# Pooled attention and a tanh-shrink layer on one core: group 2 as seven products, and another order of transfers in group 1

## The chip, the cores and the metric

The kernel runs on one core of a Trainium2 chip. The time is the device time of the program in microseconds (us). The engines are TensorE (PE, with its weight loads as PEld), VectorE (DVE), ScalarE (ACT), GpSimd (POOL) and SyncE (SP). SyncE only issues transfers here. Each engine works through its own instructions in order.

## The reference

```python
# q, k, v: (8, 8, 576, 64) float32;  w_in: (512, 2048);  w_out: (2048, 512)
k_p = k.reshape(B, H, 72, 8, D).mean(axis=3)
v_p = v.reshape(B, H, 72, 8, D).mean(axis=3)
scores = (1 / sqrt(D)) * q @ k_p.T                 # 576 x 72 for each head
attn = softmax(scores)
x = (attn @ v_p) -> rows of 8 heads x 64, (4608, 512)
h = x @ w_in
out = (h - tanh(h)) @ w_out                        # (4608, 512), float32
```

## The kernel before

The 4608 rows are worked in nine groups of 512. Groups 0 to 7 are the first 512 tokens of batches 0 to 7. The last 64 tokens of each batch (the tails, two batches to a block of 128) make up group 8. Group 0 has a part of its own, written out by hand; groups 1 to 8 are one loop over `g`.

In each turn of that loop, TensorE does the two large products of group `g`: 16 column blocks of `x @ w_in` (`h_mms`, L445, four matmuls of 128x512 to a block), and then the output product. Between these matmuls stand the small ones that make x of the next batch, `nb = g + 1`. A dictionary `plan` says after which unit of group `g` each piece stands: negative keys are the 16 column blocks, counted to the end, and keys from 0 are units of the output product. The pieces are

- "s": scores of a block of 128 tokens (`s_mms`, L311), row maximum and difference on VectorE (L323, L326),
- "e": the exponential on ScalarE (L362),
- "t": turning the weights by a DMA transpose, two blocks at a time (`e_turn_dma`, L371, tiles E and ET; El and ETl for a tail),
- "a": weights by values on TensorE (`av_mms`, L398), then the normalisation on VectorE (L419, L420),
- "x": turning x by a DMA transpose into `xT`, two blocks at a time (`x_turn_dma`, L428; `xTt` for a tail), which the first product of the next group reads.

The first product goes, two column blocks at a time, through ScalarE's tanh (L458) and a subtraction on VectorE (L459) into `gT`.

The output product has two forms. In the plain form it is 16 units of four matmuls of 128x512 (`o_mms`, L513): four row blocks, each copied out by ScalarE and stored (`o_store`, L535, L538). For the groups in `SEVEN` it is a Strassen-Winograd scheme of seven products in 14 units of eight matmuls of 128x256 (`product`, L591), with sums of `gT` (`g_sum`, L573) and of quarters of the weights. The sums of the weights are made once, by eight subtractions on VectorE (`w_sums`, L556), that the units of the plain groups pop off the list `w_ops`. A group in `SEVEN` has a plan of its own, `PLAN7`, in which the scores stand earlier and a tail's values (`tail_values`) go into the next group by way of `carry`.

Inputs for later batches come in by DMA on SyncE's queue, in the order in which the code issues them: keys, queries and values (`k_pieces`, `q_pieces`, `v_pieces`), and last tokens (`tail_pieces`). Keys are pooled on GpSimd (`pool_k`, L214 to L220), turned (`k_turn_dma`, L272, tile kT), and copied into the block layout `KB` (`k_place_kT`, L266). Queries are cast (`q_cast`, L280) and turned (`q_turn_dma`, L286, tile qT). Values are pooled into `VB` on GpSimd (`pool_v`, L229 to L256). Last tokens are cast by GpSimd (`tail_cast`, L184) and turned (`turn_tail`, L187). `stores` holds the output transfers until `run` issues them.

The PSUM banks are shared by hand: in a plain group the first product takes bank `i % 6`; in a group in `SEVEN` it takes the pairs (2, 3), (4, 5), (0, 1) in turn, while its scores stand in 6 and 7.

## Time and profile before

| | |
|---|---|
| median of 3 runs | 292.66 us (291.98 to 294.29) |
| profiled execution | 291.9 us, its span 290.2 us |
| TensorE busy | 279.5 us, 96% of the span |
| VectorE, ScalarE, GpSimd busy | 219.1, 150.5, 145.3 us |
| read from and written to HBM | 36.70 and 9.44 MB |

The profile shows one execution; its times count from the start of the span. A row of a timeline gives start, duration, engine, line and operation, and in brackets the idle time before it with what ended it. In the list of instruction groups the numbers behind the first bar are busy time in us and the mean of one in ns. A DMA row's first number is the time in which SyncE issues it; its landing is listed apart, as the time from issue to landing.

### The profile page before, as it was taken

The numbers are of one execution on the slowest core, as the hardware profiler recorded it, in microseconds if no ns is written. First come the engines' busy times: TensorE is split into PE (matmuls) and PEld (weight loads), VectorE is DVE, ScalarE is ACT, GpSimd is POOL, SyncE is SP. The second block draws the span as 40 slices with busy tenths as digits, with TensorE's granted clock in tenths as the row PEclk, the third lists the DMA queues.
The fourth block names the chain that finished last, engine by engine and source line by source line (L and its number), as shares of the span: only waits on it lengthen the run. The fifth ranks groups of instructions, "written<-read, shape, count | busy, mean of one in ns | idle before, by whom it ended". The sixth has DMA issues, their size and how long they took to land.

```text
span 290.2 us, 5474 instructions
## 1 busy us (share of the span) xinstructions
PE 279.5 (96%) x2154; PEld 179.4 (62%) x2163; DVE 219.1 (76%) x310; ACT 150.5 (52%) x226; POOL 145.3 (50%) x120
## 2 busy tenths in 40 slices
PE   6699999999999999999999999999999999999994
PEld 2489955444554455448944885488548854874583
DVE  6776876888857995599659975996599757935782
ACT  2686653366416841478366735783576336415630
POOL 7839873149411970882799279917930720010000
PEclk9999999999999999999999999999999999999999
DMA  7999999799989999888899788979622641011005
GB/s 224 231 282 273 206 263 249 149 339 270 219 224 252 328 245 175 291 228 203 166 246 292 205 173 228 304 221 165 201 48 44 95 167 21 1 75 73 0 2 145
DMA packets 84474, 54.56 MB, mean 188 GB/s; under 512 B 59904, under 2 KB 73344, under 8 KB 84448
## 3 DMA queue, kind: packets, MB, share of 16 engines
q1 hardware_dynamic: 77744, 45.17, 61.6%
q0 software_dynamic: 6320, 8.65, 14.2%
q10 hardware_dynamic: 384, 0.39, 0.5%
q8 instruction: 17, 0.28, 0.4%
q14 instruction: 9, 0.07, 0.1%
HBM read 36.70 MB, written 9.44 MB: 159 GB/s over the span
## 4 chain that ended last, share of the span: by engine, by line
PE 85%; DVE 6%; ACT 4%; DMA 2%; issue 1%; SPq 0%; ACTq 0%
PE PS L445 34%; PE PS L591 24%; PE PS L513 14%; PE PS L398 4%; PE PS L465 4%; PE PS L311 3%; DVE gT L459 3%; DMA q_raw<-in_q_dram 2%; PE PS L292 1%; DVE sh L326 1%; DVE mx L323 1%; ACT qT L701 1%; ACT t_sb L458 1%; ACT ET L381 1%; ACT E L362 1%
## 5 line engine op out<-in xcount | busy, mean ns | idle before, releaser
L445 PE MATMUL PS<-xT,w1b 128*128 128x512 bf16 x448 | 100.8, 379 | 0.0
L459 DVE TENSOR_TENSOR gT<-PS,t_sb 128x1024 bf16<-128x1024 f32 x64 | 76.8, 1219 | 28.8 <-ACT t_sb L458 28.8
L458 ACT ACTIVATE t_sb<-PS 128x1024 f32<-128x1024 f32 x64 | 65.6, 1025 | 45.6 <-PE PS L445 43.8
L445 PEld LDWEIGHTS <-w1b 128*128 128x128 bf16 x512 | 49.4, 98 | 55.2
L591 PEld LDWEIGHTS <-gT 128*128 128x128 bf16 x480 | 46.3, 98 | 5.9
L513 PE MATMUL PS<-w2b,gT 128*128 128x512 bf16 x183 | 44.7, 379 | 0.5
L591 PE MATMUL PS<-w2b,gT 128*128 128x256 bf16 x288 | 34.4, 272 | 0.0
L573 POOL TENSOR_TENSOR gT<-gT 128x1024 bf16<-128x1024 bf16 x8 | 16.8, 2120 | 29.1 <-DVE rden L419 29.1
L513 PEld LDWEIGHTS <-gT 128*128 128x128 bf16 x192 | 17.4, 98 | 17.4
L323 DVE TENSOR_REDUCE mx<-PS 128x8 f32<-128x576 f32 x35 | 26.2, 749 | 1.6 <-PE PS L311 1.6
L326 DVE TENSOR_TENSOR sh<-PS,mx 128x576 f32<-128x576 f32 x35 | 26.5, 757 | 1.2
L362 ACT ACTIVATE E<-sh 128x576 bf16<-128x576 f32 x31 | 21.2, 684 | 9.4 <-DVE sh L326 9.3
L420 DVE TENSOR_TENSOR x_sb<-PS,rden 128x512 bf16<-128x512 f32 x32 | 22.1, 692 | 1.1
L229 POOL TENSOR_TENSOR v_raw<-v_raw 128x1280 f32<-128x1280 f32 x6 | 17.4, 2900 | 7.9 <-DMA v_raw<-in_v_dram 7.8
L214 POOL TENSOR_TENSOR k_raw<-k_raw 128x1280 f32<-128x1280 f32 x6 | 17.4, 2903 | 4.0 <-DMA k_raw<-in_k_dram 4.0
L618 DVE TENSOR_TENSOR o_h<-PS,q_raw 128x256 f32<-128x256 f32 x20 | 8.5, 424 | 12.6 <-PE PS L591 11.1
L419 DVE RECIPROCAL rden<-PS 128x8 f32<-128x8 f32 x36 | 7.4, 204 | 14.0 <-PE PS L398 14.0
L625 POOL TENSOR_TENSOR o_h<-o_h,k_raw 128x512 f32<-128x512 f32 x5 | 6.4, 1271 | 21.3 <-DVE o_h L618 21.0
L535 ACT COPY o_h<-PS 128x512 f32<-128x512 f32 x10 | 5.8, 583 | 21.1 <-PE PS L513 21.1
L398 PE MATMUL PS<-VB,ET 128*128 128x130 bf16 (+2 forms) x192 | 16.3, 221 | 0.1
L465 PE MATMUL PS<-xT,w1b 128*128 128x128 bf16 x256 | 15.6, 219 | 0.3 <-ACT xT L437 0.3
L398 PEld LDWEIGHTS <-ET 128*128 128x128 bf16 x192 | 13.5, 98 | 2.9 <-ACT ET L381 0.3
(104 smaller groups left out, 364.0 us busy)
## 6 DMA issues: line engine op xcount, KB each, us to landing
k_raw<-in_k_dram SPq DMA_DIRECT2D x14, 512.0 KB, 6.0
q_raw<-in_q_dram SPq DMA_DIRECT2D x12, 512.0 KB, 6.9
v_raw<-in_v_dram SPq DMA_DIRECT2D x12, 512.0 KB, 4.8
out_dram<-o_h SPq DMA_DIRECT2D x10, 512.0 KB, 3.8
out_dram<-o_h SPq DMA_DIRECT2D x12, 256.0 KB, 3.1
w1b<-in_moe_w_in_dram POOLq DMA_DIRECT2D x4, 512.0 KB, 10.3
q_raw<-in_q_dram POOLq DMA_DIRECT2D x2, 1024.0 KB, 15.4
w2b<-in_moe_w_out_dram POOLq DMA_DIRECT2D x4, 512.0 KB, 11.2
```

The lines of the kernel that those rows point to most:

```text
L214: eng.tensor_tensor(out=r[:, :, 0:4, :], in0=r[:, :, 0:4, :], in1=r[:, :, 4:8, :], op=ALU.add)
L323: nc.vector.reduce_max(out=mx.rearrange("p k h o -> p k (h o)"), in_=sc, axis=AX.X)
L326: nc.vector.tensor_tensor(out=sh[:, :, :, :], in0=sc, in1=mx.to_broadcast([128, 2, 4, G]), op=ALU.subtract)
L362: nc.scalar.activation(out=E[:, e, :, :].rearrange("p t c -> p (t c)")[:, 0:NK], in_=sh.rearrange("p k h c -> p (k h c)"), func=ACT.Exp, s ...
L398: nc.tensor.matmul(PS[ps, banks[half], D1 * h : D1 * (h + s1 - s0)], lhsT=ET[:, t, c0 : c0 + (ps.stop - ps.start)], rhs=VB[kb][:, t, s0:s1 ...
L420: nc.vector.tensor_tensor(out=x_sb, in0=ps[:, :, :, 0:D], in1=rden.to_broadcast([128, 2, 4, D]), op=ALU.mult,)
L445: nc.tensor.matmul(PS[:, bank, :].rearrange("p (j c) -> p j c", j=R), lhsT=w1b[:, fb, i * 128 : (i + 1) * 128], rhs=xT_of(g)[:, :, fb, :], ...
L458: nc.scalar.activation(out=t_sb[:, :, :], in_=ps, func=ACT.Tanh)
L459: nc.vector.tensor_sub(out=gT[:, i : i + 2, :], in0=ps, in1=t_sb[:, :, :])
L465: mm = nc.tensor.matmul(PS[:, bank, 128 * n : 128 * n + 128], lhsT=w1b[:, fb, (4 * c + n) * 128 : (4 * c + n + 1) * 128], rhs=xT_of(0)[:, ...
L513: mm = nc.tensor.matmul(PS[:, bank, 0 : c1 - c0], lhsT=gT[:, i, tb * 128 : (tb + 1) * 128], rhs=w2b[:, i, c0:c1], start=(i == 0), stop=(i ...
L591: nc.tensor.matmul(ps, lhsT=A[:, i, 128 * b : 128 * b + 128], rhs=B_[:, i, :], start=(n in "24" and i == 0), stop=(i == NQ - 1), skip_grou ...
```

## The change

Group 2 joins the groups in `SEVEN`. With it, all eight sums of the weights are popped in group 1, at eight units in place of four, and batch 3's tail is cast at the start of group 2. That leaves group 1 as the only plain group in the loop, and what was a case for `g == 1` becomes the plan itself, with some pieces moved by a unit: blocks 2 and 3 of values from unit 10 to 9, the tail's values from 12 to 13. On SyncE's queue in group 1, values of batch 3 are issued at unit 3, before x's turns (they were issued at the end of the group); keys are turned at unit 9 (from 4) and queries at unit 10 (from 0), both behind x's turns; the last tokens are loaded behind keys and queries of batch 4. The turned keys are placed by ScalarE and not by GpSimd. Group 0 issues its four stores together; group 1 issues its first two with the third.

```diff
-SEVEN = (3, 4, 5, 6, 7, 8)
+SEVEN = (2, 3, 4, 5, 6, 7, 8)
...
             if g in SEVEN:
                 r += k_pieces(g + 2) + q_pieces(g + 2)
             else:
-                r += (v_pieces(g + 1) if g == 2 else []) + q_pieces(g + 2) + k_pieces(g + 2)
+                r += q_pieces(g + 2) + k_pieces(g + 2)
...
             o_store(0, u % 4, OB[u % 4], (se, ve)[u % 2])
-    run(stores, 2)
+    run(stores)
...
             plan = {
-                -12: [("s", 0)],
-                -9: [("e", 0)],
-                -8: [("s", 1)],
-                -5: [("e", 1), ("t", 0)],
-                -3: [("s", 2)],
+                -10: [("s", 0)],
+                -7: [("e", 0)],
+                -5: [("s", 1)],
+                -2: [("e", 1), ("t", 0)],
+                -1: [("s", 2)],
                 0: [("e", 2)],
                 1: [("s", 3)],
-                3: [("e", 3), ("t", 1)],
-                4: [("a", 0)],
-                5: [("a", 1), ("x", 0)],
+                3: [("e", 3), ("t", 1), ("s", 4)],
+                4: [("e", 4), ("t", 2)],
+                6: [("a", 0)],
+                7: [("a", 1), ("x", 0)],
                 9: [("a", 2), ("a", 3), ("x", 1)],
+                13: [("a", 4), ("x", 2)],
             }
-            if g == 1:
-                plan[-10], plan[-7], plan[-5] = plan.pop(-12), plan.pop(-9), plan.pop(-8)
-                plan[-2], plan[-1] = [("e", 1), ("t", 0)], plan.pop(-3)
             if tail is not None:
                 units.append((s_tail(tail), av_tail(tail), slot_tl))
-                plan[3].append(("s", 4))
-                plan[4] += [("e", 4), ("t", 2)]
-                if g == 1:
-                    plan[6], plan[7] = plan[4][:1], plan.pop(5)
-                    plan[4] = plan[4][1:]
-                    plan[10] = plan.pop(9)
-                plan[12] = [("a", 4), ("x", 2)]
...
-        if nb in (5, 7):
+        if nb in (3, 5, 7):
             tail_cast(tail)
...
-                if tail and n == (1 if g in SEVEN else 0):
+                if tail and n == 1:
                     turn_tail(tail)
...
             if qd == 3:
                 o_store(g, tb, 4 + tb % 2, se)
-                if g == 1 or tb > 1:
+                if tb > 1:
                     run(stores)
...
             if more:
-                if u == (0 if g == 1 else 3):
+                if u == 3:
+                    run(v_next)
+                if u == 10:
                     q_turn_dma(nb + 1)
-                if u == 0:
-                    run(stores)
-                if u == (4 if g == 1 else 9):
+                if u == 9:
                     k_turn_dma(nb + 1)
-                    k_place_kT(nb + 1, ge)
-                if u == 11 and nb % 2 == 0:
-                    run(tail_pieces(nb // 2))
-                    tail_cast(nb // 2)
+                    k_place_kT(nb + 1, se)
             if u == 13:
                 load_for(g + 1)
-            if u in (8, 9, 13, 14):
+                run(tail_pieces(nb // 2))
+            if u in (6, 7, 8, 9, 12, 13, 14, 15):
                 w_ops.pop(0)()
```

## The prediction

> **What bounds the kernel now.** I read the page first: the engines' busy time, the granted clock and the costliest group.
>
> ```profile
> span 290.2 us, 5474 instructions
> PE 279.5 (96%) x2154; PEld 179.4 (62%) x2163; DVE 219.1 (76%) x310; ACT 150.5 (52%) x226; POOL 145.3 (50%) x120
> PEclk9999999999999999999999999999999999999999
> L445 PE MATMUL PS<-xT,w1b 128*128 128x512 bf16 x448 | 100.8, 379 | 0.0
> PE 85%; DVE 6%; ACT 4%; DMA 2%; issue 1%; SPq 0%; ACTq 0%
> ```
>
> TensorE is busy for 96% of the span at the full clock, and 85% of the chain that ended last is its work. So time is won by taking matmuls out and lost wherever TensorE is made to wait. Next I cut the span at the first L445 matmul of each group (read off the chain in order of time) and asked for the busy time of each stretch. The columns are span, then PE, PEld, DVE, ACT and POOL.
>
> ```profile
> 53.97:85.60 31.63, 31.29 (x186) 15.62 (x188) 25.72 (x38) 14.81 (x18) 14.79 (x11) 1.00 0.96 252
> 85.60:116.90 31.30, 31.14 (x187) 15.61 (x188) 23.07 (x32) 15.35 (x19) 13.90 (x9) 1.00 1.00 244
> 116.90:145.36 28.46, 28.46 (x217) 19.65 (x216) 22.32 (x29) 16.92 (x26) 19.97 (x13) 1.00 0.89 221
> 145.36:174.83 29.47, 29.30 (x226) 19.74 (x224) 24.17 (x32) 18.03 (x28) 22.04 (x15) 1.00 0.89 229
> 174.83:204.04 29.21, 29.21 (x229) 20.11 (x228) 23.56 (x32) 17.43 (x28) 21.24 (x14) 1.00 0.91 226
> 204.04:233.00 28.96, 28.96 (x226) 19.82 (x224) 24.17 (x32) 16.32 (x26) 15.32 (x11) 1.00 0.44 95
> ```
>
> The rows are groups 1 to 6. Groups 1 and 2 run the plain output product; from 3 on it is the seven products. The last column but one is the DMA engines' share, and in groups 1 and 2 it is 0.96 and 1.00.
>
> **Part 1, group 2 in seven products.** The chain prices the two forms in the groups that do nothing beside them:
>
> ```profile
> 247.57 12.37 PE PS L591 x112
> 259.94 13.81 PE PS L445 x64
> ```
>
> The second row is 64 matmuls of 128x512 (the first product; the plain output product has as many of the same shape), the first is the 112 of 128x256 of the seven. The exchange gives 13.81 - 12.37 = 1.44 us. Whole groups say the same: group 6 is seven products with four blocks and a tail's scores, which group 2 becomes (28.96); group 5 carries a tail's values in, which group 3 becomes (29.21). Together 58.17, against 31.30 + 28.46 = 59.76 now. So -1.59 us, if both run as undisturbed as groups 5 and 6, whose PE is busy without a gap.
>
> The four weight sums that move from group 2 into group 1 are four more subtractions on VectorE. They are needed only by the first product of group 2, which is 14 us later. Their cover is VectorE's idle time, 31.63 - 25.72 = 5.91 us in group 1, for 4 x 0.69 = 2.8 us; without it, they would sit ahead of the normalisations, which part 2 follows.
>
> ```profile
> 76.29 0.69 DVE L420 TENSOR_TENSOR x_sb<-PS,rden 128x512 bf16<-128x512 f32 x1
> 78.83 0.69 DVE L556 TENSOR_TENSOR k_raw<-w2b,k_raw 128x1024 bf16<-128x1024 bf16 x1
> 80.21 0.21 DVE L419 RECIPROCAL rden<-PS 128x8 f32<-128x8 f32 x1 [0.69 <-PE PS L398]
> 81.30 0.69 DVE L420 TENSOR_TENSOR x_sb<-PS,rden 128x512 bf16<-128x512 f32 x1
> ```
>
> **Part 2, the end of group 1 on the DMA queue of SyncE.** This is where it is decided. SyncE issues in order, so I list what it does there now:
>
> ```profile
> 62.32 1.01 SPq L538 DMA_DIRECT2D out_dram<-o_h  x2
> 69.15 2.06 SPq L371 DMA_TRANSPOSE ET<-E  x1
> 71.31 1.94 SPq L286 DMA_TRANSPOSE qT<-q_bf  x1
> 74.96 1.34 SPq L371 DMA_TRANSPOSE ET<-E  x1
> 78.31 1.23 SPq L272 DMA_TRANSPOSE kT<-kd  x1
> 80.73 2.65 SPq L428 DMA_TRANSPOSE xT<-x_sb  x2
> 86.81 1.79 SPq L136 DMA_DIRECT2D v_raw<-in_v_dram  x2
> ```
>
> Queries and keys of batch 3 are turned at 71.31 and 78.31, both ahead of x. After the change the order is ET, values of batch 3 (three loads), the tail's ET, x, x, kT, qT, stores, the tail's x, keys and queries of batch 4, last tokens. The second turn of x is issued when VectorE has normalised the fourth block. TensorE reaches blocks three and four a unit earlier (0.86 us), but three weight sums (2.1 us) now stand ahead, where one or two fitted into gaps: starting each operation when the one before ends, from the first normalisation at 76.29, gives 81.6 to 82.0, the same place as now (81.30 + 0.69 = 81.99). Each turn keeps SyncE 1.2 us, qT 1.9 to 2.1, so kT is issued at about 83.1 and qT at about 84.4, which is 13 us later than now. Their landing times are:
>
> ```profile
> L286 SPq DMA_TRANSPOSE qT<-q_bf x5: 1907/2072/2469, 52.0 to 167.7; - x5
> DMA to landing us min/median/max: 4.3/4.4/5.5
> L272 SPq DMA_TRANSPOSE kT<-kd x5: 1201/1227/1267, 55.1 to 172.9; - x5
> DMA to landing us min/median/max: 2.6/2.6/3.5
> ```
>
> So kT lands at 85.7 to 86.6 and qT at 88.7 to 89.9. The values ahead of them can add to it. They go out from 76.3, when the ET of 74.96 is issued, the last of the three at about 77.5. Of the same three loads of batch 2 the last was issued at 57.45 and landed 4.7 us later, at 62.15, and the small turn behind them landed at 58.06 + 4.5 = 62.56:
>
> ```profile
> 57.45 0.51 SPq L142 DMA_DIRECT2D v_raw<-in_v_dram  x1
> v_raw<-in_v_dram SPq DMA_DIRECT2D x1, 128.0 KB, 4.7
> 58.06 1.22 SPq L187 DMA_TRANSPOSE tl_T<-tl_bf  x1
> tl_T<-tl_bf SPq DMA_TRANSPOSE x1, 4.5
> ```
>
> By this the values land at about 82.2 and the tail's ET at about 82.7, ahead of its use near 83.1. The queue goes on with x, x, kT and qT, 37 squares of 128x128. With 11 squares more, qT takes 1.8 us longer than kT, 0.16 us a square, so the 37 take 6 us and qT is there at 88.7 at the earliest by this count too. With the slowest kT and qT of the rows (0.9 and 1.1 us over their medians) it is 90.7. I take 89.6, near the middle, since both the queue and the slowest single turns speak for some delay.
>
> When does TensorE want qT? Group 2 begins at 85.60 if group 1 keeps its length, and as a group of seven it computes scores after three column blocks of its first product, where it now does after five:
>
> ```profile
> 85.60 4.32 PE PS L445 x20
> 146.86 0.89 ACT L266 COPY KB<-kT 64x288 bf16<-64x288 bf16 x2 [2.83 <-DMA kT<-kd]
> 148.88 1.23 DVE L459 TENSOR_TENSOR gT<-PS,t_sb 128x1024 bf16<-128x1024 f32 x1 [3.00 <-ACT t_sb L458]
> 165.24 1.05 PE L591 MATMUL PS<-v_raw,q_raw 128*128 128x256 bf16 x8 [0.17 <-DVE q_raw L573]
> 85.64 0.59 ACT L535 COPY o_h<-PS 128x512 f32<-128x512 f32 x1 [3.62 <-PE PS L513]
> 87.42 1.02 ACT L458 ACTIVATE t_sb<-PS 128x1024 f32<-128x1024 f32 x1 [1.19 <-PE PS L445]
> ```
>
> 12 of those matmuls take 2.59 us (4.32 x 12 / 20), so the scores are wanted at 88.19: with qT at 89.6, a stall of 1.4 us.
>
> The same stall is fed from the other side. ScalarE now places kT, in its own order: behind that wait stand two output copies (0.59 each) and the first tanh of group 2. With kT at 86.1: 0.89 + 1.18 + 1.02 us make the first subtraction on VectorE start at about 89.3, against 88.47 (87.42 + 1.02) now. Bank 4, which the third column block needs, is copied out by 87.6, wanted at 87.3. In group 4 the chain from the first subtraction (148.88) to the second half of product 7 (165.24) is VectorE's own work throughout, 16.36 us; 89.3 + 16.4 = 105.7, and TensorE would be there 19.9 us after the start less the 0.5 of group 4's loss, at 105.0. So 0.7 us from that side alone. The two overlap; the larger counts: +1.4, bounds 0.5 and 2.5. None is below nothing, since qT at its fastest is 88.7.
>
> **Part 3, the rest.** Four stores of group 0 go in one go instead of two and two: 0.5 MB more ahead of the ET of 69.15, which at group 1's 252 GB/s is 2.1 us of queue.
>
> ```profile
> ET<-E SPq DMA_TRANSPOSE x1, 4.0
> 75.65 0.36 PE PS L398 x6
> ```
>
> That ET landed 4.0 us after its issue, at 73.2, and its first reader is at 75.65. So the cover is 2.5 us, and I count nothing; without it, every microsecond of it is on the path. The values of batch 3 land 9 us sooner, but only GpSimd waits for them; no TensorE row does. Behind ScalarE's copies waits the store of the third block, and behind that store on SyncE stand the tail's x, keys, queries and last tokens of batch 4, from about 89 on. GpSimd's pooling of keys and ScalarE's query casts in group 2 wait for these, half a group later; I count nothing for it, and if that cover is gone the casts stand ahead of the last tanh. Group 3 now starts with kT placed by ScalarE, as group 4 does, which lost 29.47 - 28.96 = 0.5 us to it, group 5 nothing: +0.2, bounds 0 and 0.5.
>
> **Sum.** -1.59 + 1.4 + 0.2 = 0.0 (by the bounds -1.1 to +1.4) on the profiled execution of 291.9 us (span 290.2): about 291.9. The runs shown have a median of 292.66 and a lowest of 291.98, so the profiled one is at the fast end; I put the forecast at 292.3, between the two.
>
> [...]
>
> **Rivals.** (a) Forecast: a gain of 1.6 us is mostly paid back at the first scores of group 2: as median 291.5 to 293.1, chance 0.48.
>
> (b) The turns land in time. If qT lands by 88.2, as it would if squares overlap with their issue (kT lands 1.4 us after its issue ends), or 0.5 us later, at the fastest of its row, the sum is 291.9 - 1.59 = 290.3 to 290.8; as median 290.7 to 291.2. For it: SyncE's queue is otherwise empty then. Against: qT never took under 4.3. Chance 0.27. [...]
>
> (c) Slower: the values in front hold up the x turns. If the values and the tail's ET land 1 us later than I count, at 83.7, the second x (16 squares, 2.6 us) lands at 86.3, after the 85.60 at which the first product of group 2 wants it, kT at 87.1 and qT, 1.1 us slow as its slowest row, at 90.8: a stall of 2.6 us, and 0.5 in group 3, in sum +1.5: 293.4, as median 293.8. It decides for slower from a qT later than 89.6. For it: DMA share 0.96 and 1.00 here. Against: the loads that now stand there (batch 3's) have 10 us of slack behind them. Chance 0.20.
>
> (d) The change doesn't do what it says: VectorE sets the pace of group 2, so that it stays at 31.30 while group 3 gains the tail's values (29.21 - 28.46): +0.75, 292.7, as median 293.1. Against it: groups 3 to 6 do not show this. Chance 0.05.
>
> **How the numbers follow.** One per cent, 2.9 us, is about what a measurement of this kernel can tell from no change. No case gains that: even -1.59 with nothing lost is 0.5%, so faster 0.03. Slower by that needs a stall of over 4 us, or (c) with something more: 0.08. Within: 0.89. The range takes (b) and (c) in: 290.6 to 294.2.
>
> **What would show it.** Right: the first qT-fed score matmul of group 2 with an idle before it of about 1.4 us, released by the DMA of qT; ScalarE idle for kT at about 86; groups 2 and 3 together 59.8 us. Wrong: no idle there and the pair near 58.2 (b), or group 2's first product late (c). The forecast fails most simply if qT lands 1 us sooner or later than 89.6.

## The result, and the profile after

The changed kernel takes 295.23 us as median of ten runs (294.0 to 297.19), the kernel before 292.70 (291.93 to 294.29). The ratio is 1.0086, with an interval of [1.0058, 1.0114]: slower by 0.9%. The forecast of 292.3 was 2.9 us too low, and the upper end of its range, 294.2, was passed by 1.0 us.

The page of the kernel after, in three rows: span, engines, and the chain that ended last by engine.

```profile
span 293.5 us, 5595 instructions
PE 279.0 (95%) x2211; PEld 183.7 (63%) x2211; DVE 227.5 (78%) x316; ACT 154.0 (52%) x237; POOL 153.8 (52%) x121
PE 75%; DMA 10%; ACT 6%; DVE 4%; issue 2%; SPq 1%; ACTq 0%
```

TensorE is busy for 0.5 us less in a span that is 3.3 us longer, and the DMA's part of the chain has gone from 2% to 10%. The same cut by groups as before shows where (groups 1 to 4; columns as there, the last but one is the DMA share):

```profile
54.43:86.60 32.17, 31.67 (x189) 15.71 (x190) 28.12 (x41) 14.33 (x18) 17.48 (x12) 1.00 0.94 250
86.60:118.98 32.38, 29.31 (x226) 19.64 (x224) 27.52 (x34) 18.91 (x30) 18.82 (x12) 1.00 1.09 228
118.98:148.50 29.52, 29.40 (x230) 20.02 (x228) 23.55 (x32) 17.31 (x28) 21.25 (x14) 1.00 0.97 222
148.50:177.81 29.31, 28.95 (x224) 19.64 (x222) 24.41 (x33) 17.98 (x28) 21.69 (x14) 1.00 1.02 235
```

In group 2 TensorE works 29.31 us, 1.8 less than before, and still the group takes 32.38, 1.1 more than before. So 3.07 us of it are waits, where there were 0.16. The list of what TensorE waits for from 50 us on names them (total, times, longest, in us):

```profile
PE PS L311 <- DMA qT<-q_bf: 1.7, 1, 1.7
PE PS L398 <- DMA ET<-E: 1.4, 1, 1.4
PE PS L445 <- DMA xT<-x_sb: 0.7, 2, 0.4
PE PS L398 <- DMA ETl<-El: 0.3, 1, 0.3
PE PS L311 <- DVE sh L326: 0.2, 1, 0.2
```

And the timeline of TensorE has the three that fall into groups 1 and 2 (start, duration, in brackets the idle time before it):

```profile
84.06 0.72 PE L398 MATMUL PS<-VB,ETl 128*64 128x130 bf16 x12 [0.32 <-DMA ETl<-El]
...
90.87 0.42 PE L311 MATMUL PS<-KB,qT 128*128 128x144 bf16 x4 [1.67 <-DMA qT<-q_bf]
...
112.37 0.53 PE L398 MATMUL PS<-VB,ET 128*128 128x130 bf16 x6 [1.40 <-DMA ET<-E]
```

The first scores of group 2 wait 1.67 us for the queries' turn, as forecast. The 1.40 us at 112.37, where the third block of weights meets the values, stand in no step of the prediction. SyncE's rows show when both turns went out:

```profile
77.00 1.16 SPq L136 DMA_DIRECT2D v_raw<-in_v_dram  x2
78.21 0.48 SPq L142 DMA_DIRECT2D v_raw<-in_v_dram  x1
78.78 1.23 SPq L371 DMA_TRANSPOSE ETl<-El  x1
80.11 3.63 SPq L428 DMA_TRANSPOSE xT<-x_sb  x2
83.84 1.23 SPq L272 DMA_TRANSPOSE kT<-kd  x1
85.12 1.83 SPq L286 DMA_TRANSPOSE qT<-q_bf  x1
...
106.60 1.61 SPq L371 DMA_TRANSPOSE ET<-E  x1
```

The chain in order of time has both, with the time from issue to landing:

```profile
85.12 5.71 DMA qT<-q_bf
...
106.60 5.72 DMA ET<-E
```

The queries' turn is issued 0.7 us after the forecast time, but group 1 itself starts 0.6 us later in this trace (54.43 against 53.80), so by the group's own time it is late by 0.1. It needs 5.71 us, where the median before was 4.4. The turn of weights needs 5.72, where the turns at the same place in groups 3 to 6 of the kernel before landed after 3.4 to 3.8. Why these two turns are so late is the question that most of the experiments go after.

With a group's length taken as the time from its first L445 matmul to that of the next group, the loss from group 1 on is all in groups 1 to 3:

| group | 1 | 2 | 3 | 4 | 5 | 6 |
|---|---|---|---|---|---|---|
| before | 31.64 | 31.30 | 28.46 | 29.46 | 29.22 | 28.95 |
| after | 32.02 | 32.37 | 29.52 | 29.47 | 29.23 | 28.96 |
| the prediction's terms | 31.64 | 30.36 | 29.41 | as before | as before | as before |

Groups 1 to 3 take 93.91 us together, 2.51 more than before. Another 0.63 us of the 3.3 stand ahead of group 1; in a second trace of the kernel after, group 1 starts at 53.85, so that they aren't shown to be the change's. (The ends of the windows above were read off a few matmuls later, so that these lengths differ from theirs by up to 0.16 us.)

### The profile page after: what moved, and what is told of

Its sections match the earlier page's. It is cut to its first block, busy times and chain, and to the rows that moved or that the text cites. A ratio compares the mean times of both kernels' runs of the same rounds, so it can differ in the third digit from the quotient of the medians.

```text
span 293.5 us, 5595 instructions
## 1 busy us (share of the span) xinstructions
PE 279.0 (95%) x2211; PEld 183.7 (63%) x2211; DVE 227.5 (78%) x316; ACT 154.0 (52%) x237; POOL 153.8 (52%) x121
## 4 chain that ended last, share of the span: by engine, by line
PE 75%; DMA 10%; ACT 6%; DVE 4%; issue 2%; SPq 1%; ACTq 0%
PE PS L445 35%; PE PS L591 23%; PE PS L513 5%; PE PS L465 4%; PE PS L398 4%; DMA ET<-E 3%; PE PS L311 3%; DMA xT<-x_sb 2%; DMA q_raw<-in_q_dram 2%; DMA qT<-q_bf 2%; PE PS L292 1%; ACT q_bf L280 1%; DVE x_sb L420 1%; ACT E L362 1%; ACT t_sb L458 1%
## 5 line engine op out<-in xcount | busy, mean ns | idle before, releaser
L445 PE MATMUL PS<-xT,w1b 128*128 128x512 bf16 x448 | 100.8, 379 | 0.7 <-DMA xT<-x_sb 0.7
L445 PEld LDWEIGHTS <-w1b 128*128 128x128 bf16 x512 | 49.3, 98 | 56.2 <-issue 0.8
L591 PEld LDWEIGHTS <-gT 128*128 128x128 bf16 x560 | 53.9, 98 | 6.9
L591 PE MATMUL PS<-w2b,gT 128*128 128x256 bf16 x336 | 40.1, 273 | 0.0
L573 POOL TENSOR_TENSOR gT<-gT 128x1024 bf16<-128x1024 bf16 x10 | 21.0, 2121 | 32.8 <-DVE rden L419 32.8
L513 PE MATMUL PS<-w2b,gT 128*128 128x512 bf16 x128 | 30.6, 379 | 0.0
L618 DVE TENSOR_TENSOR o_h<-PS,q_raw 128x256 f32<-128x256 f32 x22 | 9.3, 423 | 13.5 <-PE PS L591 13.5
L625 POOL TENSOR_TENSOR o_h<-o_h,k_raw 128x512 f32<-128x512 f32 x6 | 7.6, 1274 | 21.4 <-DVE o_h L618 21.0
L513 PEld LDWEIGHTS <-gT 128*128 128x128 bf16 x128 | 11.5, 98 | 11.1
L311 PEld LDWEIGHTS <-qT 128*128 128x128 bf16 x128 | 10.0, 98 | 9.8 <-DMA qT<-q_bf 2.2
```

What stands on the lines that cost most here:

```text
L445: nc.tensor.matmul(PS[:, bank, :].rearrange("p (j c) -> p j c", j=R), lhsT=w1b[:, fb, i * 128 : (i + 1) * 128], rhs=xT_of(g)[:, :, fb, :], ...
L513: mm = nc.tensor.matmul(PS[:, bank, 0 : c1 - c0], lhsT=gT[:, i, tb * 128 : (tb + 1) * 128], rhs=w2b[:, i, c0:c1], start=(i == 0), stop=(i ...
L573: return eng.tensor_tensor(out=o, in0=x, in1=y, op=op)
L591: nc.tensor.matmul(ps, lhsT=A[:, i, 128 * b : 128 * b + 128], rhs=B_[:, i, :], start=(n in "24" and i == 0), stop=(i == NQ - 1), skip_grou ...
```

## The experiments

Some expectations name the theories by letters. A: the turns at the end of group 1 go out too late. B: batch 4's loads, now ahead of the turns of group 2, hold these up. C: the seven products are themselves the cost. D: the load on the DMA engines, stores above all, lengthens the turns. P: VectorE and GpSimd hinder each other. F: a packet of the queue that the profile calls instruction, taken for one that brings TensorE its instructions, lengthens the turn in flight. Q: it is only the order in SyncE's queue, and what each turn waits for there, that makes the turns late. The table gives the medians (before was 292.56 to 292.92 beside them), the ratios to the kernel before with their intervals, and the groups' lengths in the profiled execution.

| kernel | median us | ratio | groups 1, 2, 3, 4 |
|---|---|---|---|
| after | 295.23 | 1.0086 [1.0058, 1.0114] | 32.02, 32.37, 29.52, 29.47 |
| queries early | 293.89 | 1.0034 [1.0016, 1.0052] | 32.15, 31.23, 29.63, – |
| seven products alone | 294.31 | 1.0057 [1.0036, 1.0079] | 31.64, 32.42, 29.30, – |
| values of batch 4 behind | 296.67 | 1.0124 [1.0093, 1.0155] | 31.82, 33.00, 31.44, – |
| order alone | 294.95 | 1.0061 [1.0039, 1.0083] | 31.86, 32.59, 28.46, – |
| after, without stores | 294.06 | 1.0050 [1.0030, 1.0070] | 32.25, 31.58, 29.56, – |
| before, without stores | 292.72 | 0.9999 [0.9980, 1.0018] | 31.64, 31.29, 28.47, – |
| seven alone, without stores | 294.11 | 1.0055 [1.0034, 1.0077] | 31.63, 33.79, 29.22, – |
| keys and queries early | 294.80 | 1.0079 [1.0056, 1.0102] | 32.57, 31.73, 29.55, – |
| after, shifted by 64 | 294.79 | 1.0066 [1.0037, 1.0095] | 32.23, 29.93, 30.10, 29.83 |
| before, shifted by 64 | 293.93 | 1.0033 [1.0014, 1.0052] | 32.36, 31.29, 29.66, 29.37 |
| keys and queries early, shifted | 295.24 | 1.0080 [1.0051, 1.0108] | 32.96, 31.16, 29.68, 29.96 |
| after, shifted by 32 | 295.58 | 1.0094 [1.0068, 1.0120] | 35.75, 29.16, 30.28, – |
| after, shifted by 96 | 294.65 | 1.0066 [1.0042, 1.0089] | 32.02, 30.26, 29.56, 28.95 |
| values of batch 3 late | 296.98 | 1.0140 [1.0119, 1.0161] | 31.63, 35.48, 29.66, – |

### The parts of the change

**Queries turned early.** Only the queries' turn goes back to unit 0 of group 1.

```diff
+                if u == 0:
+                    q_turn_dma(nb + 1)
                 if u == 3:
                     run(v_next)
-                if u == 10:
-                    q_turn_dma(nb + 1)
```

> The changed kernel with one edit: queries of batch 3 are turned at unit 0 of group 1 (as before the change), not at unit 10 behind x's turns. Theory A (the queue of SyncE is late from the end of group 1 on, and the late turn of queries is the piece that makes it so): the 1.67 us idle before the first scores of group 2 goes, keys and queries of batch 4 are issued some 1.8 us sooner, and the 1.40 us idle before the third block of values in group 2 shrinks to under 0.5: about 292.5. Rival B (that second idle comes from the values of batch 4, which stand straight ahead of the second ET whatever came earlier): only the first idle goes, 293.5. Rival C (seven products in group 2 are themselves the cost): no change by more than 0.5 us, 295.

The wait for qT is gone and the median falls by 1.34 us, most of the 1.67, to near rival B's 293.5. So theory A holds for this one wait. The other stays, at the same place and with a turn issued at the same time (106.55):

```profile
111.85 0.53 PE L398 MATMUL PS<-VB,ET 128*128 128x130 bf16 x6 [0.99 <-DMA ET<-E]
```

It is therefore no consequence of the queries' stall.

**Seven products without the new order.** From the kernel before: group 2 in `SEVEN`, the eight weight sums in group 1, everything on SyncE as it was (batch 4's keys go ahead of its queries).

```diff
-SEVEN = (3, 4, 5, 6, 7, 8)
+SEVEN = (2, 3, 4, 5, 6, 7, 8)
...
-            if u in (8, 9, 13, 14):
+            if u in (6, 7, 8, 9, 12, 13, 14, 15):
```

> The kernel before with only group 2 put into the seven products and all weight sums made in group 1; the transfers in group 1 keep the order of before (queries turned at unit 0, keys at unit 4 and placed by GpSimd, values of batch 3 loaded at the end, stores in two and two). Theory A (the order is the cost, the products the gain): groups 2 and 3 together take 58.2 to 59 us, 1.0 to 1.6 less than before, no idle before the first scores: 291.2 to 291.8. Rival C (the products cost): groups 2 and 3 over 60 us, over 293.5. A third way: the values of batch 3 now come too late for a group of seven, GpSimd ends its pooling late, the tail's turn holds up SyncE, and there is an idle at the end of group 2: 292 to 293.

No stall of queries, and yet group 2 is not shorter: waits of 1.05 us for a turn of weights, 0.47 for a sum on GpSimd, 0.53 for x. With values of batch 3 loaded at the end of group 1, GpSimd pools them only from 94.69, and its keys then run beside VectorE's sums:

```profile
94.69 2.91 POOL L229 TENSOR_TENSOR v_raw<-v_raw 128x1280 f32<-128x1280 f32 x1 [12.32 <-DMA v_raw<-in_v_dram]
...
105.42 1.86 POOL L217 TENSOR_TENSOR k_raw<-k_raw 128x640 f32<-128x640 f32 x1
107.37 2.40 POOL L220 TENSOR_TENSOR kd<-k_raw 128x640 bf16<-128x640 f32 x1
```

The last two take 1.54 to 1.55 each in all groups of the kernel before. So the old order does not suit seven products either. The time is the one of rival C (over 293.5), but TensorE works 29.79 us in group 2, less than the 31.14 before; the rest are waits.

**The order without seven products.** From the kernel before: the transfers and the plan as in the kernel after, group 2 still plain.

```diff
-                if u == (0 if g == 1 else 3):
+                if u == 3 and g == 1:
+                    run(v_next)
+                if u == (10 if g == 1 else 3):
                     q_turn_dma(nb + 1)
...
-                if u == (4 if g == 1 else 9):
+                if u == 9:
                     k_turn_dma(nb + 1)
-                    k_place_kT(nb + 1, ge)
...
+                    k_place_kT(nb + 1, se if g == 1 else ge)
...
             if u == 13:
                 load_for(g + 1)
+                if g == 1:
+                    run(tail_pieces(nb // 2))
```

> The kernel before with only the new order of transfers in group 1 (values of batch 3 at unit 3, keys turned at unit 9 and placed by ScalarE, queries turned at unit 10, last tokens at the end, group 0's stores in one go); group 2 stays plain, with its scores after five column blocks. Theory A with the interplay (the order costs because a group of seven wants its scores 1.7 us sooner and its values 3 us sooner): 0 to +1 us against before, 292.7 to 293.7. If the order costs by itself whatever group 2 is: +2.5 us or more, 295. If nothing waits, 292.7.

A plain group 2 wants its first scores two column blocks later, and the wait for qT is gone. What comes in its place is a wait for the last tokens, which are now loaded behind everything else:

```profile
105.74 0.45 PE L311 MATMUL PS<-KB,tl_T 128*64 128x144 bf16 x8 [1.00 <-DMA tl_T<-tl_bf]
```

By the ratios the two parts cost 1.7 and 1.8 us by themselves and 2.5 together; neither is free.

**Values of batch 3 late, values of batch 4 behind.** Two kernels from the kernel after. In one, batch 3's values go out at the end of group 1 (unit 13), so that keys and queries have SyncE's queue for themselves. In the other, batch 4's values go out at unit 13 of group 2.

```diff
-                if u == 3:
-                    run(v_next)
...
             if u == 13:
+                run(v_next)
                 load_for(g + 1)
```

> The changed kernel with the values of batch 3 loaded at the end of group 1, ahead of keys and queries of batch 4 (as before the change), all else as changed. If the values ahead of x are what delays keys and queries: the turn of queries is issued at the same 85 us but lands under 4.6 us after it, the idle falls from 1.67 under 0.8. If not, it stays over 1.2. Either way the values come at 98 and later for a group that wants them pooled at 106, and GpSimd's pooling meets VectorE's sums in the products: group 2 stays over 32, 295 or more.

```diff
             if u == 13:
                 k_place_kT(nb + 1, se)
+                run(v_next)
                 load_for(g + 1)
...
-        if g > 1:
+        if g > 2:
             run(v_next)
```

> The changed kernel with one edit: in group 2 the values of batch 4 are loaded at unit 13, behind ET, x, keys, and not ahead of the second ET. Rival B (these 1.18 MB ahead of the second ET are the cause of its 5.7 us): that ET lands in under 4.5 us and the 1.40 us idle before the third block of values goes, the 1.67 us idle stays: about 293.9. Theory A (the queue is late from group 1 on): the idle shrinks only in part, 294.6. Loads that come this late may cost in group 3, which would show as an idle there.

Both are slower. Without the values in front the queries' turn is issued at 83.81, 1.3 us sooner, of which 0.75 is that group 1 starts sooner in this trace (53.68). It lands after 5.6 us, and the wait for it is still 1.38 us. So taking the values away doesn't take this wait away. By itself that doesn't clear them, since this turn too has an instruction packet beside it (at 85, in a table below). The list of waits shows what the late values cost instead, for values of batch 3:

```profile
PE PS L398 <- DMA ET<-E: 4.3, 3, 2.6
```

and for values of batch 4, where the turns of group 2 were to gain:

```profile
PE PS L398 <- DMA ET<-E: 2.3, 3, 1.2
```

Of these three, one is group 2's turn of the third block: it lands after 5.1 us and is waited for by 0.80 in place of 1.40. Theory B had it under 4.5 with no wait, so the values are at most a part of this cause. The other two are in group 3, where the values are now late.

**Keys and queries early.** The first of these experiments, and the keys turned at unit 4 and placed by GpSimd as before.

```diff
-                if u == 9:
+                if u == 4:
                     k_turn_dma(nb + 1)
-                    k_place_kT(nb + 1, se)
+                    k_place_kT(nb + 1, ge)
```

> The changed kernel with queries turned at unit 0 and keys at unit 4, placed by GpSimd, as before the change; values of batch 3 still ahead of x. Theory Q: with no turn behind x left but the tail's, all three idles at the start of group 2 go and the gain comes out, 291.5 to 292. Theory D: one idle is traded for another as in the run with queries early alone; groups 1 to 3 stay over 92.3 us, 293 to 294.

With no turn of batch 3's keys and queries left at the end of group 1 the wait for ET is still 0.93 us in group 2, and the tail's turn in group 1 is waited for longer (0.65). The median is 0.9 us worse than with the queries alone.

### Load on the DMA engines

Three kernels leave out the eight stores of groups 0 and 1: the kernel after, the kernel before as a control, and the seven products alone.

```diff
-        for r0, r1, dst in out_rows(g, tb):
+        for r0, r1, dst in out_rows(g, tb) if g > 1 else []:
```

> The changed kernel without the eight stores of groups 0 and 1 (2.1 MB; those rows of the output are not written), all else in place. Theory D (the 16 DMA engines are the bound from 54 to 118 us, where their share is 0.96 and 1.00 already before the change, so a group 2 that is 1.6 us shorter has nothing to run on): the load falls by some 7 us of their time, ET and the loads land sooner, the 1.40 us idle of group 2 goes and the idle for queries shrinks; groups 1 to 3 fall from 93.9 to under 92.3, 292.5 or less. Rival Q (a chain: VectorE's normalisation, then x, keys, queries in one queue): the queries are issued at 85 us as before whatever the engines carry, both idles stay within 0.5 us, 294.5 to 295.

> The control: the kernel before without the same eight stores (those rows are not written). TensorE waited for no DMA there, so both theories expect no change: groups 1 to 3 at 91.2 to 91.4 us, 292.2 to 292.8. If it gains over 1 us, leaving out stores does something else as well, and the run above has to be read against this one.

> Group 2 in seven products with the old order of transfers, without the same eight stores (those rows are not written). Theory D: with the DMA engines relieved the gain of the seven products comes out: groups 1 to 3 at 90.3 to 91, 291.2 to 291.8, against 93.36 with the stores. Rival P (the loss there comes from VectorE and GpSimd getting in each other's way in group 2, 1.22 us sums taking 2.4 us): it stays over 92.5, 293.5.

The control does not move (0.9999). The kernel after gains 1.2 us, but both waits stay: 1.43 us for qT and 0.86 for ET. They land after 5.5 and 5.2 us. So the stores take part, above all in the second wait, and are not the main cause: the 292.5 of theory D did not come. The seven products alone gain nothing measurable, and in their profile the largest wait is for GpSimd's sum, which had gone behind the late values and keys:

```profile
116.07 1.48 PE L591 MATMUL PS<-k_raw,gT 128*128 128x256 bf16 x12 [1.74 <-POOL gT L573]
```

That fits theory P, for the seven products in the old order only; how much of it is VectorE in GpSimd's way, and how much the late loads, is not shown. In the kernel after TensorE waits for no sum of GpSimd's.

### What lengthens the two turns

The queue "q8 instruction" has 17 packets of 16 KB (0.28 MB in all), in both kernels. The kernel after has 4422 TensorE instructions (2211 matmuls and as many weight loads), one packet for 260 of them if all are its own. In slices of 1 us, the traces show one packet in flight with each of the two long turns. Here are 85 to 91 us and 106 to 112.5 us of the kernel after (packets, MB, share; then transfer, count, us from issue to landing):

```profile
q8 instruction: 1, 0.02, 1.0%
...
qT<-q_bf SPq DMA_TRANSPOSE x1, 5.7
...
q8 instruction: 1, 0.02, 1.0%
...
ET<-E SPq DMA_TRANSPOSE x1, 5.7
```

The slices with a packet, in us of the span:

| kernel | packets at |
|---|---|
| before | 48 69 86 109 130 144 164 179 197 211 227 |
| after | 48 69 88 110 129 142 160 174 195 207 225 |
| after, shifted by 64 | 55 75 102 113 135 146 167 186 200 215 230 |
| before, shifted by 64 | 56 76 100 117 139 158 172 192 203 225 235 |
| after, shifted by 32 | 44 61 83 108 120 140 158 173 190 203 223 |
| after, shifted by 96 | 49 74 95 112 130 142 164 175 197 211 228 |
| values of batch 3 late | 48 69 85 111 130 144 163 175 197 209 228 |

The queries' turns, all of one size, can be set beside these times. In the kernel before they are issued at 51.99, 71.31, 106.77, 136.36, 167.70 and 194.37 us and land after 4.3, 4.4, 5.5, 4.7, 4.4 and 5.6 us. Packets fall into the third (109) and the sixth (197), and into no other. In the kernel after, the turn of 85.12 with the packet of 88 takes 5.7; four others take 4.3 to 4.8, one of them (138.52) with the packet of 142 in its last half microsecond. One is in between: the turn of 109.66 lands after 4.9, though the packet of 110 comes just behind its issue. That packet is also the one beside the late ET, which was issued 3 us earlier.

All twenty traces together say when a packet costs. Of their 120 turns of queries, 68 had no packet that began while they were in flight: they landed after 4.2 to 5.7 us, the median 4.4. In 22 a packet began 1.3 to 4.0 us after the issue: 4.6 to 6.7 us, the median 5.6, all but one over 5.2. In nine it began within the first 0.6 us, as with the turn of 109.66: 4.3 to 4.9, the median 4.4. (The other 21 had one later than 4.0 us, which a turn that lands early can't meet.) So a packet in the middle of the flight costs about 1.2 us, and one at its start next to nothing.

The busy share of the 16 DMA engines from 85 to 91 us, in 40 slices of 0.15 us, shows what happens. The first row is the kernel after; the second is the same kernel with its packets moved, as in the next experiment, out of this stretch (its third trace):

```profile
DMA  9999991006999999999999999900010001999999
DMA  9999991006999999999999999999999998999999
```

The rows are alike up to 88.9. Then the engines of the kernel after stand nearly idle for 1.2 us (88.9 to 90.1, at 0 to 34 GB/s where about 210 stood before), just behind the packet of 88, with the queries' turn still in flight. So the turn isn't slowed by a lack of engines; it is held. What holds it in the meantime, the profile doesn't show.

To move the packets and nothing else, 64 small matmuls were added to the ones that run at the start, while TensorE waits for its first data. With their weight loads that is 128 of the 260 instructions to a packet, about half its spacing.

```diff
-    fill(11, 7)
+    fill(3, 7)
+    for _ in range(72):
+        nc.tensor.matmul(
+            PS[0:64, 7, 0:64], lhsT=zeros[:, 0:64], rhs=zeros[:, 0:64], start=True, stop=True
+        )
```

> The changed kernel with 64 more small matmuls on zeros at the start (3 wide and 72 of 64 columns in place of 11 wide), while TensorE waits for the first loads. Nothing else changes, but every later 16 KB packet of the queue that the profile calls instruction comes 64 matmuls sooner. Theory F (such a packet, seen at 88 and 110 us, sits in the DMA engines while the queries' turn and the second ET are in flight and makes them land 1.2 to 1.5 us later): the packets come at about 74 and 103, the queries land 4.3 to 4.7 us after issue and the second ET in under 4.2, the idle of 1.67 falls under 0.7, that of 1.40 to 0 to 0.3, group 2 takes 30.7 or less instead of 32.4, and the time falls to 292.7 to 293.7. Rival Q (order of transfers alone): both idles stay within 0.4 us, 295.

> The kernel before with the same 64 small matmuls more at the start. Theory F: its packets, now at 109, 130, 144, 164 and 179, move to about 95, 116, 137, 157 and 169; the one at 137 meets group 3's second ET (wanted 0.5 us after it lands), the one at 169 the x turns of group 4: idles of 0.5 to 1.0 us appear in group 3 or at the start of group 5, and the time rises by 0.5 to 1.5 us, 293.2 to 294.2. Rival Q: no idle, 292.5 to 292.9.

With 64 matmuls of TensorE more ahead of them, the packets of 88 and 110 are now at 75 and 102, and that of 129 is at 113: 8 to 16 us sooner. qT, issued at 84.84, lands after 4.4 us, and its wait falls from 1.67 to 0.31. The ET of the third block lands after 4.6 and is not waited for at all:

```profile
86.18:116.11 29.93, 29.47 (x226) 19.52 (x224) 27.41 (x34) 19.00 (x30) 18.80 (x12) 1.00 1.05 242
116.11:146.21 30.10, 29.57 (x231) 19.94 (x230) 23.56 (x32) 17.33 (x27) 21.24 (x14) 1.00 0.84 222
```

Group 2 is 2.4 us shorter than in the kernel after, and TensorE's waits in it are down to 29.93 - 29.47 = 0.46 us. But groups 3 and 4 are 0.6 and 0.4 us longer, with new waits for ET (0.43 and 0.72). So the waits went as theory F had them, and the time did not: 294.79 is near rival Q's 295, and the intervals do not tell it from the kernel after.

In the kernel before it goes the other way. Its packets fell where turns had slack, and moved they do not: the ET of group 3 that meets the packet at 139 lands after 5.3 us where it took 3.7, and TensorE waits. From 135 to 142 us:

```profile
q8 instruction: 1, 0.02, 0.8%
...
ET<-E SPq DMA_TRANSPOSE x1, 5.3
```

```profile
141.30 0.53 PE L398 MATMUL PS<-VB,ET 128*128 128x130 bf16 x6 [1.02 <-DMA ET<-E]
```

The median of the kernel before rises by 1.0 us, as theory F had it, with nothing changed but 64 matmuls in an opening wait. Two more shifts of the kernel after, by 32 and by 96 matmuls, and the early turns shifted by 64:

> The changed kernel with 32 small matmuls more at the start. Theory F, from the places of the packets in the changed kernel (88, 110): they move to about 81 and 107. The one at 107 still meets the second ET of group 2 (issued 106.6), the one at 81 the tail's ET and x of group 1, the queries are clear: the idle for queries falls under 0.7, that for the second ET stays 0.7 or more, an idle of 0.6 or more stands before the tail's values or the start of group 2; group 2 takes 30.3 to 31.6. Rival (the shift by 64 helped for another reason, as a warmer or colder start): group 2 as with 64, 29.9.

> The changed kernel with 96 small matmuls more at the start. Theory F: the packets of 88 and 110 move to about 71 and 97, that of 129 to 114, where it meets the x turns of group 2. Both idles of group 2 go as with 64 (group 2 in 30.4 or less), and an idle of 0.4 to 1.0 stands at the start of group 3, for x. Rival: group 2 over 31.5.

> The version with queries turned at unit 0 and keys at unit 4, placed by GpSimd (294.8 as it was), with the same 64 small matmuls more at the start. Theory F: the second ET of group 2 no longer meets a packet at 109, its 0.93 us idle goes; the 0.95 us of waits on VectorE at 92 to 94 stay: groups 2 and 3 in 60.2 or less instead of 61.3, 293.2 to 294. Rival Q: no change, 294.8.

With either shift qT lands after 4.3 us and the ET of group 2's third block is not waited for; group 2 takes 29.16 and 30.26. With 32, the packet at 83 meets the tail's turn instead:

```profile
86.16 0.72 PE L398 MATMUL PS<-VB,ETl 128*64 128x130 bf16 x12 [2.04 <-DMA ETl<-El]
```

and group 1 takes 35.75. Part of that is not the wait itself: eight plain matmuls behind this wait took 3.42 us, where they take 1.89 elsewhere, with a granted clock of 0.85 between 80 and 90 us. Theory F had put a wait of 0.7 us or more before the third block here, and missed: the packet is at 108, 0.4 us behind the issue of that turn, which lands after 3.7 us all the same. That is the packet at the start of a flight, as above. With 96, a packet at 197 costs group 5 a wait of 1.04 us for an ET, beside 0.59 for a copy of keys, and the group takes 31.70 in place of 29.23; the wait for x that was expected at the start of group 3 did not come, since x, with the packet of 112 beside it, landed 0.1 us ahead of its use. With keys and queries early and the shift by 64, the wait for ET in group 2 is gone, and waits of up to 0.82 us for turns come up in other groups. Groups 2 and 3 take 60.84 us, where theory F had 60.2 or less, and the median is 295.24, where it had 293.2 to 294: no gain, as rival Q had it.

### Does a packet keep its place?

The profile of the shifted kernel after was the fastest of its twelve runs: 293.28 us, against a median of 294.79. So four more traces were taken, of the kernels as they are.

> The changed kernel once more, for a second trace. If the places of the instruction packets are fixed by the program (theory F in its strict form), the waits are those of the first trace: the queries' turn about 1.4 to 1.7 us before the first scores of group 2, a turn of weights about 1.4 us at the third block of values, span 293 to 294. If they drift by a few microseconds from execution to execution, one of the two waits is under 0.5 us and another turn is waited for.

> The changed kernel with the 64 extra matmuls at the start once more. Its first trace had 291.6 us of span, while the median of its executions is 1.5 us higher. Strict F: again 291.6, group 2 at 29.9, groups 3 and 4 at 30.1 and 29.8. Drifting packets: a span of about 293, with other turns waited for in groups 1 to 5, 1 to 2 us more in sum.

> The same kernel a third time, to tell a drift from a single odd trace: strict F gives the same waits in all three, drift gives three different sets with spans between 291.6 and 295.

> The kernel before once more. Strict F: no wait of TensorE for a turn over 0.3 us, groups 1 to 3 at 91.4 us in sum, span 290 to 291. Drift: a wait of up to 1 us appears in one of the groups 3 to 8, while groups 1 and 2 stay, since their turns are issued long before they are wanted.

The packets keep their places within about 1 us (87 and 110 in the kernel after; 102 and 114, then 103 and 113 shifted); in the kernel before they differ by up to 2.3. In the kernel after both waits come again, behind landings of 5.5 and 5.7 us:

```profile
90.59 0.42 PE L311 MATMUL PS<-KB,qT 128*128 128x144 bf16 x4 [1.61 <-DMA qT<-q_bf]
...
112.29 0.53 PE L398 MATMUL PS<-VB,ET 128*128 128x130 bf16 x6 [1.56 <-DMA ET<-E]
```

In the shifted kernel qT lands after 4.4 us in all three traces, and its wait is 0.31, 0.38 and 0.35. Group 2 is not the same each time. Its rows in the second and the third trace:

```profile
86.31:117.69 31.38, 29.72 (x226) 19.51 (x224) 29.09 (x35) 19.00 (x30) 19.47 (x13) 1.00 1.02 236
```

```profile
86.45:116.74 30.29, 29.30 (x226) 19.59 (x225) 27.74 (x34) 19.07 (x30) 18.76 (x12) 1.00 1.07 241
```

The packet at 102 to 103 now meets the turn of the first two blocks, issued at 97.62 to 97.93. It lands after 7.3 to 8.1 us, where it took 6.2 in the kernel after, and is waited for by 0.64 us in the third trace. In the second trace TensorE waits for VectorE there (0.60 and 0.29 us). So strict F is right for the kernel after, and for the shifted one only in the place of its packets. Group 2 takes 30.53 us as mean of three, 1.9 less than the 32.45 of the kernel after's two traces; groups 3 and 4 take 60.0 against 59.0. Over groups 1 to 4 the net is 0.8 us; it agrees in sign with the medians, which differ by 0.44.

Before, traced again, had one wait of 0.52 us for an ET in group 2, where neither reading expected any. The packets account for it as theory F would: in the first trace that ET landed at 108.91, just ahead of the packet of 109.1; in the second, issued 0.3 us later, it met the packet at 108.8 and landed after 5.36 us in place of 3.55.

## Why the prediction was wrong

**The time, step by step.** Its terms give 91.41 us for groups 1 to 3; measured were 93.91. Of the missing 2.50, group 2 has 2.01, group 1 0.38, group 3 0.11. The 2.01 are 1.40 for the turn of weights, 0.27 more for the queries, and 0.34 by which TensorE's own work in group 2 (29.30) is longer than group 6's (28.96).

**Part 1, right in the exchange of products.** TensorE's busy time in group 2 falls by 1.8 us, where 2.2 would reach group 6's 28.96. Where the shifts take the two long waits away the group is at 29.2 to 31.4 us. The gain is there and is paid away.

**Part 2, right in place, short by 0.3, and near in part by luck.** The wait at the first qT-fed scores was put at 1.4 us and is 1.67 and 1.61 in two traces. kT was put at 86.1, and ScalarE's copy of it starts at 86.49. Counted from the start of group 1, qT was issued 0.1 us later than forecast and took 0.5 longer than the 5.2 us from 84.4 to 89.6; but group 2, which wants it, also began 0.4 later, and the two errors nearly cancel. The landing time was taken from its row of 4.3, 4.4 and 5.5 us as a scatter, to be met by a value in the middle. By the packets' times it isn't scatter: the 5.5 is the turn of 106.77, with the packet of 109 beside it. Read that way, the row had two prices, and the question was where the next packet falls. In the shifted kernel, at the lower price, the wait is 0.3 to 0.4 us.

**The step that failed: the turns of weights in group 2, counted at nothing.** Part 1 took the gain "if both run as undisturbed as groups 5 and 6", whose PE is "busy without a gap". Part 3 ("half a group later; I count nothing for it") looked at GpSimd and ScalarE as those that wait in group 2, and never at the turns of weights there. Group 2's ET of the third block is issued at 106.60, wanted at 110.97 and lands at 112.32. It had 4.37 us. The 3.4 to 4.6 us of the shifted traces would have cost 0.2 at most; 5.72 costs 1.40. No row was quoted for the cover of this turn, and there was next to none. The kernel before shows it: in its groups 3 to 6, all in seven products, the turn at this place was wanted 4.2 us after its issue and landed after 3.4 to 3.8. That is 0.4 to 0.8 us of cover, in group 3 by these rows (issue, landing, first reader):

```profile
135.05 1.27 SPq L371 DMA_TRANSPOSE ET<-E  x1
ET<-E SPq DMA_TRANSPOSE x1, 3.7
139.25 0.52 PE L398 MATMUL PS<-VB,ET 128*128 128x130 bf16 x6
```

None of these four turns met a packet in the middle of its flight. Another turn of weights in group 3 did (issued at 127.69, the packet of 130), and landed after 5.0 us; it had 7.35 us, so that nothing waited.

**Group 1, taken as unchanged.** The tail's turn is issued at 78.78, behind three loads of values, and is waited for by 0.32 us in both traces of the kernel after. The sum of "about 82.7, ahead of its use near 83.1" left 0.4 us of cover. The turn took 5.2 us, 0.7 more than the 4.5 that was counted.

**The side chain of VectorE, right in time for another reason.** The first subtraction of group 2 was put 3.7 us after the group's start (89.3 against 85.60; the terms given add up to 89.2), behind ScalarE's copy of kT. It starts at 90.16, 3.7 us after 86.45. But ScalarE's tanh had ended at 89.44. What stands ahead of the subtraction on VectorE is three weight sums, which are in no term of this chain. They run beside GpSimd's pooling of values:

```profile
85.67 1.35 DVE L556 TENSOR_TENSOR k_raw<-w2b,k_raw 128x1024 bf16<-128x1024 bf16 x1
86.94 2.03 DVE L556 TENSOR_TENSOR v_raw<-w2b 128x1024 bf16<-128x1024 bf16 x1
88.89 1.34 DVE L556 TENSOR_TENSOR v_raw<-w2b,k_raw 128x1024 bf16<-128x1024 bf16 x1
90.16 1.21 DVE L459 TENSOR_TENSOR gT<-PS,t_sb 128x1024 bf16<-128x1024 f32 x1
```

```profile
86.55 1.88 POOL L232 TENSOR_TENSOR v_raw<-v_raw 128x640 f32<-128x640 f32 x1
88.50 1.19 POOL L235 TENSOR_TENSOR v_raw<-v_raw 128x320 f32<-128x320 f32 x1
```

They take 4.72 us; three at the 0.68 to 0.69 us that each takes in the kernel before would take 2.0 to 2.1. No wait of TensorE in group 2 is put down to VectorE in the kernel after. Where qT is in time, there are such waits near 106 us: 0.28 and 0.28 with the queries early, 0.60 and 0.29 in one trace of the shifted kernel. Whether they come from these sums isn't shown.

**The rivals.** (b), turns in time, is what the shifts come near to in group 2. (c) came nearest in its time, with 293.8, but not by its cause: x landed at 85.80, ahead of the 86.45 at which it was wanted, and in the shifted kernel, with the values where they are, qT lands after 4.4 us. (d) did not happen. The chance of 0.89 for a change within 1% came true, at its edge, but not by the small terms that it stood on; and the measurement tells 0.9% from no change, where the prediction thought one per cent was the least.

**What stays open.** The shifts move waits as the packets would have it, in both kernels and both directions, and that a packet can lengthen the turn in flight by 1.1 to 1.6 us is shown by that. Why the engines then stand idle is open. And the medians follow the packets' places only in part: no shift of the kernel after comes within 1.5 us of the kernel before. The groups of seven products have little slack around their turns wherever a packet falls, and whether some place of the packets would leave all of them free was not found. Nor is it known how much of the 1.2 us without stores is queueing and how much the turns' own rate. A kernel with fewer TensorE instructions in groups 1 and 2, hence, at one for about 260, fewer packets, wasn't tried. No version beat the kernel before.

## What to carry to other kernels

A DMA turn that is issued 4.1 us ahead of its reader, with a landing time of 4.4 us, isn't hidden (the queries' turn of the shifted kernel after, waited for by 0.31 us): look for the slack of every turn in the new schedule, not only of those that the change moves, and take the slowest landing of the row as the price until something else explains it. When the landings of one kind of transfer fall into two clumps, look at what else is on the DMA engines at the slow ones, the instruction queue too. And a change of under one per cent that alters the number of TensorE instructions is best measured together with a version that has some idle instructions more at the start, since a kernel's standing can rest by a microsecond on where its instruction packets fall (1.0 us, the kernel before shifted by 64).

## What the runs showed of the hardware

- A 16 KB packet of the queue "q8 instruction", 17 of them beside 4422 TensorE instructions, one for about 260, made the DMA turn in flight with it land late: over twenty traces, queries after 5.6 us (median of 22) when the packet began 1.3 to 4.0 us behind their issue, against 4.4 without one (median of 68) and 4.4 with one in the first 0.6 us (median of nine). A turn of weights landed after 5.7 us against 3.4 to 4.6, and after 5.3 against 3.7 in the kernel before.
- Behind such a packet (at 88 us in the kernel after) the 16 DMA engines stood nearly idle for 1.2 us, with a turn still in flight and stores queued behind it.
- 64 small matmuls in an opening wait made the kernel before slower by 1.0 us (ratio 1.0033, [1.0014, 1.0052]).
- Three weight sums on VectorE, 0.68 to 0.69 us each in the kernel before, took 1.34 to 2.03 us beside GpSimd's pooling (from 85.67 us on, in the kernel after), and that pooling 1.88 and 1.19 for 1.54 and 0.86. In the trace both lose, by 0.3 to 1.4 us an instruction; by what, it doesn't show.
